# Linear attention, SwiGLU and softplus layers on one core: one more unit's output products by seven, and gate and value partials kept in tiles

## The chip, the cores and the metric

The kernel runs on one core of a Trainium2 chip. The metric is the device time of one execution in microseconds, and of several executions the median. The core's engines run beside each other and wait for one another by semaphores: TensorE (PE, with its weight loads PEld), VectorE (DVE), ScalarE (ACT), GpSimd (POOL) and SyncE (SP), whose queue issues all transfers here.

## The reference, cut to what matters

```python
q_s = softmax(q, axis=-1); k_s = softmax(k, axis=2)           # 4 batches, 8 heads, 576 rows, 64 wide
kv = einsum('bhsd,bhse->bhde', k_s, v)
x = einsum('bhsd,bhde->bhse', q_s, kv)                         # to 2304 tokens x 512
xn = x / sqrt(mean(x * x) + 1e-6) * rms_g
g = xn @ w_gate; val = xn @ w_val                              # 512 -> 1536
x = (g / (1 + exp(-g)) * val) @ w_out                          # first layer, 1536 -> 512
h = x @ w_in                                                   # second layer, 512 -> 2048
out = (maximum(h, 0) + log1p(exp(-abs(h)))) @ w2_out           # softplus, 2048 -> 512
```

## The kernel before, in words

All data are 32-bit floats. To multiply them on TensorE, a tile is cut into two halves, a rounded one (`[:, 0]`) and the rest (`[:, 1]`), and one product is three matmuls (`mm3`, lines 946 to 948): high by high, high by low, low by high. Sums stay in the eight banks of PSUM; `bank()` hands one out.

Tokens are taken in blocks of 384 (T), two blocks to a pair, three pairs. The first layer does a third of its hidden width plainly (steps G, V, S, A, O) and the rest, and the whole second layer, "by seven": a two by two product of blocks is made from seven block products of sums and differences instead of from eight. For that, quadrants of the tokens (`quad_sum`, `quad_h`, `quad_l`) and of the weights (`pair_sum`, `make_h`, `make_l`) are summed and cut in halves ahead of time; weights prepared so are put into DRAM ("kept") and loaded again (`load_b`, line 1291).

A first-layer unit u (12 of them) is one token pair and one pair of hidden chunks. For gate and for value it makes seven products (`a_mul`, step M.u.k.g or M.u.k.v, k from 0 to 6, each six matmuls of 384 columns). Partial sums are copied (`a_copy`, step C, lines 1228 and 1232), added (`a_sum`, D, line 1236), and go through silu (SI, line 1244) and gate (U, line 1252). In the kernel before, product 0 is copied from its bank to a second bank, and product 1 is summed onto that copy; product 3 takes a third bank. The four results are cut in halves (BH, line 1264; BL, line 1268) and multiplied with the output weights onto a copy of the running output (OP, line 1272; OM; OC, line 1281).

A second-layer unit u (0 to 23, eight for each of three token pairs) makes seven products with w_in (`h_mul`, step H), copies and adds partials (HC, line 1306; HD, line 1310), and applies softplus (SP, line 1324). Its output products are either plain (`y_mul`, step Y.u.o.f.t: for two token blocks o, two hidden chunks f and three groups t of 128 tokens, 12 products of three matmuls of 512 columns, summed in six banks over the units) or by seven (`y_part`, step YP.u.k.t: 21 products of three matmuls of 256 columns). By seven needs seven tiles in halves instead of four, four sums of softplus tiles (SU, line 1371), the weights' differences (yc and yd) and, for products 1 to 4, an addition to running totals on chip (YA, line 1409); products 5 to 7 stay in five banks over all units of a token pair. In the end YX (line 1471) joins totals and banks, YS (line 1475) adds what plain units left in banks, and YO stores (lines 1357 and 1360). Which units go by seven stands in `BY7`: before, 4 to 21; units 0 to 3, 22 and 23 are plain.

The front part is the attention: q maxima, exponentials and sums (Q0 line 802, QS 806, QR 824, QM 835), k maxima (K0, line 687), transposes and broadcasts (K1, KM, K2, KS), key by value products (K3), their scaling (K4, lines 786 to 789), the attention output (X0, line 873), and the conversion of weights that come as 64-bit floats (CA, CL line 508, CD lines 514 to 522, CC, CS line 540).

What runs when is written out by hand or by a search: the text ORDER lists about 4,100 steps, and each engine does its own in that order. A step's last letter names the engine where there is a choice (V is DVE, A is ACT, P is POOL). HOMES lists which buffer each tile takes (`ps`: banks; `w`: 16 weight buffers).

Of the kernel before, what the change touches and what calls it, by code (L numbers as in the profile page):

```python
# [27 lines left out]
LQ.0.0 Q0.0.0 LQ.0.1 QS.0.0.1.V LQ.0.2 F.5 QS.0.0.0.P QE.0.0.1 Q0.0.1 Q0.0.2 LK.0.0.1 QE.0.0.0 LK.0.1.1 QS.0.1.0.P  # L28
QS.0.1.1.P MX CA.5.A LK.0.2.2 F.0 QE.0.1.0 QR.0.0 QI.0.0 LX.0 QE.0.1.1 K0.0.0.1.1.V QM.0.0.0.V QS.0.2.0.P QR.0.1 QM.0.0.1.P
K0.0.1.1.1.V K0.0.0.1.2.V K0.0.2.2.1.V F.3 K0.0.0.1.3.V QE.0.2.0 K0.0.2.2.2.V QI.0.1 B.0.33 T.1 CL.5.V K0.0.1.1.2.V F.10 MV  # L30
K0.0.2.2.3.V T.0 LQ.1.0 K0.0.1.1.3.V K0.0.0.1.4.V K0.0.1.1.4.V K0.0.2.2.4.V CA.0.A CL.0.V B.1.6 K1.0.0 CA.3.A LW.0 KM.0.0
B.2.2 K2.0.0 CD.0.0 LV.0.0.4 CL.3.P LV.0.4.8 K1.0.2 QR.0.2.0 QM.0.1.0.P KS.0.0 KE.0.0 QI.0.2.0 KM.0.2 Q0.1.0 QM.0.2.0.P
B.3.7 K2.0.2 TC.1.A KS.0.2 QS.1.0.0.P CD.3.0 CA.10.A CL.10.V QM.0.1.1.V T.2 F.6 CD.0.1 KE.0.2 MK CD.5.0 LK.1.0.2 QE.1.0.0
CD.10.0 CD.3.1 QS.1.0.1.V B.4.4 K3.0.0 LG CD.0.2 K3.0.2 TC.0.A T.3 TC.2.A LK.1.2.2 CD.3.2 K4.0.0 CC.3.A CD.10.1 K4.0.2
QE.1.0.1 QR.1.0 B.5.1 X0.0.1 T.4 X0.0.0 CA.6.A CD.10.2 LX.1 CL.6.V SQ.0.1 LQ.1.1 K0.1.0.2.1.V CD.5.1 CS.3.P SQ.0.0
K0.1.0.2.2.V K0.1.2.2.1.V X0.0.3 X0.0.2 SQ.0.2 SQ.0.3 XG.0.1.A K0.1.0.2.3.V XG.0.0.A X1.0.4.0 K0.1.2.2.2.V XG.0.2.A CC.10.A
CC.0.A X1.0.4.2 K0.1.0.2.4.V K0.1.2.2.3.V QI.1.0 X1.0.4.1 QM.1.0.1.P K0.1.2.2.4.V K1.1.0 LV.1.0.4 KM.1.0 B.6.1 K1.1.2 K2.1.0
XD.0 TC.4.A XP.0 Q0.1.1 XG.0.3.A QM.1.0.0.P KM.1.2 B.7.2 K2.1.2 X2.0 KS.1.0 T.5 KE.1.0 QS.1.1.0.P QS.1.1.1.P QE.1.1.1 LW.1
KS.1.2 F.1 X3.0.1 QE.1.1.0 X3.0.0 HH.0.0.A T.6 CS.10.P KE.1.2 LV.1.4.8 HH.0.1.A TC.3.A TC.5.A LK.2.2.2 X3.0.2 CS.0.V
HH.0.2.A F.7 HL.0.0.P B.8.1 K3.1.0 G.1.0 K3.1.2 QR.1.1 CD.6.0 LQ.2.0 X3.0.3 CA.1.A QI.1.1 QM.1.1.1.V K4.1.0 HH.0.3.A G.0.0  # L40
K4.1.2 X0.1.2 HL.0.1.P X0.1.3 CD.6.1 HL.0.2.P CA.7.A X0.1.0 K0.2.2.2.1.V CD.5.2 K0.2.2.2.2.V CL.7.V X0.1.1 SQ.1.1 XG.1.2.A
T.8 CD.6.2 HL.0.3.V SQ.1.2 CD.7.0 CL.1.V LX.2 SQ.1.0 K0.2.2.2.3.V F.4 CD.7.1 XG.1.1.A SQ.1.3 G.1.1 K0.2.2.2.4.V LK.2.0.2
XS.1.2.3.V G.0.1 G.1.2 XS.1.0.1.V G.0.2 QM.1.1.0.P XG.1.0.A V.3 CA.4.A CC.6.A G.0.3 CD.7.2 T.7 Q0.2.0 G.1.3 XG.1.3.A
K0.2.0.2.1.V CS.6.P TC.7.V K1.2.2 LW.2 G.2.0 S.1 KM.2.2 F.9 XS.1.0.2.P LQ.2.1 TC.6.A TC.8.A S.0 K0.2.0.2.2.V G.2.1 CC.5.A
CL.4.V X1.1 CC.7.A LV.2.0.4 K0.2.0.2.3.V CS.7.P X0.2.1 CD.1.0 K0.2.0.2.4.V X0.2.2 XD.1 CD.4.0 K1.2.0 K2.2.2 KM.2.0 G.2.2
CS.5.P KS.2.2 K2.2.0 KS.2.0 CA.9.A X0.2.3 X0.2.0 CD.1.1 SQ.2.1 SQ.2.2 F.2 KE.2.0 QS.2.0.0.V V.2 CL.9.V CD.1.2 XG.2.1.A
XG.2.0.A LV.2.4.8 QS.2.0.1.V CC.1.A CD.9.0 Q0.2.1 G.2.3 XP.1 X2.1 XG.2.2.A KE.2.2 CD.9.1 SQ.2.0 CD.4.1 K3.2.0 CA.2.A CS.1.P
CD.9.2 CD.4.2 CL.2.V QE.2.0.1 LX.3 F.8 CC.9.A CC.4.A LV.3.0.4 CS.9.V V.0 SQ.2.3 QE.2.0.0 X3.1.0 HH.1.0.A A.0 CS.4.P X3.1.3
XG.2.3.A K3.2.2 S.2 QS.2.1.1.P QR.2.0 G.3.0 K4.2.2 QI.2.0 QS.2.1.0.P AH.0.A V.1 HL.1.0.P HH.1.3.A K4.2.0 G.3.1 X3.1.2 LQ.1.2
X3.1.1 F.11 A.1 QM.2.0.1.P QE.2.1.1 XS.2.0.1.V G.5.0 AH.1.V G.7.0 HH.1.1.A CA.11.A HL.1.1.V G.3.2 QM.2.0.0.P G.4.0 HH.1.2.A  # L50
HL.1.2.V QE.2.1.0 T.10 CL.11.V G.3.3 S.3 G.6.0 G.7.1 CD.2.0 XS.2.2.3.V CA.8.A TC.10.A CD.2.1 LK.3.0.2 Q0.1.2 CL.8.V HL.1.3.V
CD.8.0 AL.1.V AL.0.V CD.2.2 G.7.2 CD.8.1 G.6.1 G.5.1 V.5 A.3 G.5.2 A.2 CC.2.A G.5.3 CD.8.2 T.9 CD.11.0 TC.9.A QS.1.2.0.V
QR.2.1 CD.11.1 K0.3.0.2.1.V S.5 LV.3.4.8 G.4.1 G.4.2 CC.8.A G.6.2 G.4.3 CS.2.P O.0 O.1 S.4 AH.2.A K0.3.0.2.2.V AH.3.A
XS.2.0.2.V X1.2 LQ.3.0 AL.2.V CD.11.2 G.6.3 CS.8.P K0.3.0.2.3.V XD.2 G.7.3 A.5 XP.2 QI.2.1 CC.11.A F.15 LK.3.2.2 V.4 CS.11.V
F.12 K0.3.0.2.4.V Q0.3.0 QM.2.1.0.P S.6 CA.15.A X2.2 AL.3.P X3.2.0 HH.2.0.A O.2 O.3 CA.12.A AH.5.A K1.3.0 CL.15.V A.4 S.7
E.0.2.A CD.15.0 T.11 V.7 X3.2.2 CL.12.V TC.11.A X0.3.0 QM.2.1.1.P X0.3.1 K0.3.2.2.1.V AH.4.V LQ.3.1 E.0.1.A E.0.0.V X0.3.3
KM.3.0 CD.12.0 AL.4.P QE.1.2.0 HL.2.0.P X3.2.1 XG.3.3.A XG.3.0.A QS.3.0.1.V X3.2.3 V.6 X0.3.2 SQ.3.3 Q0.3.1 CD.15.1 AL.5.P
E.0.3.A CD.12.1 A.6 SQ.3.1 O.4 SQ.3.0 AH.6.A K0.3.2.2.2.V HH.2.3.V CD.15.2 CD.12.2 AL.6.V QS.3.1.1.V QS.3.0.0.P ST.15
XG.3.1.A O.5 HH.2.1.V A.7 SQ.3.2 K0.3.2.2.3.V O.6 K2.3.0 QE.3.0.1 G.9.0 AH.7.A XS.3.0.1.P XS.3.2.3.V AL.7.V HH.2.2.A
QE.3.0.0 QE.3.1.1 O.7 XG.3.2.V KS.3.0 XS.3.0.2.P KE.3.0 E.1.0.A ST.12 X1.3 K0.3.2.2.4.V F.14 QR.1.2.0 F.19 HL.2.3.V XD.3  # L60
T.12 HL.2.1.V G.8.0 G.10.0 CA.14.A G.10.1 K1.3.2 G.9.1 CA.19.A G.8.1 HL.2.2.P CL.14.V QR.3.0 CL.19.V CD.14.0 KM.3.2 QI.3.0
LW.3 G.10.2 TC.12.V G.10.3 QI.1.2.0 QM.3.0.0.P QS.3.1.0.P XP.3 V.9 QE.3.1.0 G.9.2 T.14 G.8.2 E.1.2.V G.9.3 G.8.3 QR.3.1
TC.14.A G.11.0 QM.1.2.0.V CD.19.0 S.8 CD.19.1 K2.3.2 K3.3.0 CD.14.1 CD.19.2 F.13 S.9 A.9 KS.3.2 CD.14.2 X2.3 QI.3.1 K4.3.0
V.8 G.11.1 G.11.2 X3.3.3 QM.3.1.1.V QM.3.1.0.V T.13 G.11.3 ST.19 F.16 AH.9.V A.8 KE.3.2 T.16 S.10 QM.3.0.1.P K3.3.2 X3.3.1
AH.8.V X3.3.2 E.1.1.A V.11 K4.3.2 S.11 V.10 TC.13.A CA.13.A ST.14 T.17 CL.13.V X0.4.3 CA.16.V HH.3.1.V CD.13.0 X0.4.2
CL.16.V AL.9.P XG.4.3.A CD.16.0 X3.3.0 X0.4.0 AL.8.P A.10 T.15 SQ.4.3 X0.4.1 CD.13.1 HH.3.2.V SQ.4.2 HH.3.0.A A.11 CD.13.2
E.1.3.A ST.13 TC.17.V CD.16.1 XG.4.2.A XG.4.0.A O.8 TC.15.A SQ.4.0 HH.3.3.V HL.3.0.V CD.16.2 O.9 G.13.0 XG.4.1.A HL.3.1.V
F.18 SQ.4.1 AH.10.A HL.3.3.V XS.4.2.3.P TC.16.V F.17 AL.10.P O.10 AH.11.V AL.11.V X0.5.2 XS.4.0.1.P XS.4.0.2.P X1.4 G.14.0
XD.4 HL.3.2.P O.11 XG.5.2.V XP.4 G.13.1 CA.18.A CL.18.V G.14.1 G.13.2 G.13.3 E.2.0.A X0.5.0 SQ.5.2 ZS.1.t1.P SQ.5.0 CD.18.0
X2.4 S.13 ST.16 G.12.0 XG.5.0.A CA.17.A E.2.1.V G.12.1 CD.18.1 E.2.2.A X3.4.3 ZS.1.t3.P X0.5.3 CD.18.2 X3.4.1 V.12 E.2.3.A  # L70
V.14 X3.4.2 XG.5.3.V SQ.5.3 X0.5.1 ST.18 HH.4.1.A XG.5.1.V XS.5.2.3.P V.15 X3.4.0 V.13 SQ.5.1 G.15.0 G.15.1 HH.4.0.V
HL.4.0.P G.12.2 XS.5.0.1.V XS.5.0.2.P A.13 G.12.3 CL.17.V CD.17.0 X1.5 XD.5 CD.17.1 G.14.2 G.18.0 G.14.3 XP.5 G.19.0 S.12
HH.4.3.A HH.4.2.A G.15.2 S.14 X2.5 A.12 TU.12 HL.4.1.P G.17.0 HL.4.2.V F.22 AH.12.V LATE AL.12.P CD.17.2 WH.12.1.A G.15.3
TU.13 A.14 F.21 ZH.0.22.qe1.A G.16.0 G.16.1 S.15 ST.17 HL.4.3.V G.19.1 G.16.2 AH.13.A X3.5.3 G.19.2 AL.13.P PS.13.0.P G.18.1
ZH.0.11.qe0.V V.19 A.15 AH.14.V AL.14.V CA.21.A G.19.3 G.16.3 X3.5.2 G.17.1 V.17 X3.5.1 PS.13.1.P G.18.2 S.16 G.17.2 G.18.3
CL.21.V HH.5.1.A PS.13.2.V WH.13.2.A AH.15.V ZL.0.22.V S.19 WL.13.2.V CD.21.0 CD.21.1 G.17.3 A.19 CA.22.V WL.12.1.V HH.5.3.A
X3.5.0 CL.22.P AL.15.P V.18 S.17 HL.5.3.P CD.22.0 CD.22.1 PS.13.3.P AH.19.A HL.5.1.V O.12 CD.22.2 CD.21.2 O.13 V.16
WH.13.4.V AL.19.V O.14 WH.13.3.A O.15.0 HH.5.0.A O.15.3 A.16 O.15.2 HL.5.0.P G.20.0 G.20.1 AH.16.V AL.16.V ZS.0.t3.V TU.14
A.17 ST.21 O.16.0 HH.5.2.V HL.5.2.P S.18 V.20 TU.15 E.3.3.A PS.15.0.P G.20.2 G.20.3 ST.22 AH.17.V G.21.0 AL.17.V A.18
PS.15.1.P WH.14.1.V F.20 G.23.0 E.3.0.V PS.15.2.V ZL.0.11.V E.3.2.V G.21.1 WH.15.2.V F.23 S.20 A.20 G.21.2 O.16.3 WL.14.1.V  # L80
G.23.1 PS.15.3.V O.16.2 AH.18.A G.22.0 WL.15.2.V O.17.2 CA.23.A WL.13.3.V O.17.3 G.21.3 TU.16 ZS.0.t1.V G.22.1 AL.18.V
G.22.2 CL.23.P O.15.1 O.16.1 CD.23.0 CA.20.V E.3.1.V G.23.2 CD.23.1 AH.20.A CL.20.V CD.23.2 ST.23 G.22.3 S.22 ZH.0.21.hl.V
# [260 lines left out]
ps 3630365756452437170231547546252162513523223623322632636266234063023564  # L343
qh 01010101
qm2_ 01010101
raw 01010101011010101001010110101010101010101001010101001010101010100011010101100101011101101010
qs2_ 01201201
mx 01010101
qn 012102010210210210
# [19 lines left out]
def linear_attention_swiglu_softplus_kernel(  # L369
# [23 lines left out]
    T = 384  # L393
# [51 lines left out]
    def bank():  # L445
        return take(ps_p, "ps", [P, 512])
# [1136 lines left out]
```

## Time and profile before

| | |
|---|---|
| median of 3 runs | 885.22 us (885.11 to 886.08) |
| the profiled execution | 885.05 us |
| its span, from first to last instruction | 883.3 us |
| granted TensorE clock, mean | 0.996 |
| busy: PE, PEld, DVE, ACT, POOL | 867.8, 846.6, 759.4, 446.2, 321.7 us |
| matmuls | 5360 |

The span is what the profile shows of the profiled execution; its own time is 1.75 us longer. Busy time counts an engine's instructions; matmuls overlap each other, and their ends are modelled.

### The profile page before, as it was taken

How to read it: one execution, taken by the hardware profiler on the slowest of the kernel's cores; microseconds unless marked ns; L12 is line 12 of the kernel's file. 1: busy time of each engine (PE TensorE's matmuls, PEld its weight loads, DVE VectorE, ACT ScalarE, POOL GpSimd, SP SyncE). 2: the span in 40 equal slices, each digit the busy share in tenths (PEclk: the TensorE clock that was granted, in tenths of full speed). 3: DMA queues.
4: the chain of work that ended last, by engine and by line, in shares of the span. 5: the costliest groups of instructions: out<-in, count | busy, mean ns of one | idle time of the engine just before them, and what ended most of it. 6: DMA issues, size and time to landing. Idle time of an engine off the chain costs nothing.

```text
span 883.3 us, 15104 instructions
## 1 busy us (share of the span) xinstructions
PE 867.8 (98%) x5360; PEld 846.6 (96%) x5360; DVE 759.4 (86%) x1444; ACT 446.2 (51%) x888; POOL 321.7 (36%) x286
## 2 busy tenths in 40 slices
PE   7899999999999999999999999999999999999997
PEld 7789999999999999999999998999999999999996
DVE  7999988488898899998999999899998786877774
ACT  3578555232576654655556776757653323232220
POOL 5443522452405133131333224135325335364321
PEclk9899999999999999999999999999999999999999
DMA  9996324113889897898898989898979887678832
GB/s 259 206 250 162 96 78 127 65 49 118 297 333 362 283 349 269 306 336 323 293 359 301 351 303 339 320 323 309 333 237 341 270 292 257 211 243 298 280 100 72
DMA packets 119803, 223.03 MB, mean 253 GB/s; under 512 B 31024, under 2 KB 75824, under 8 KB 119728
## 3 DMA queue, kind: packets, MB, share of 16 engines
q1 hardware_dynamic: 119728, 222.07, 75.3%
q8 instruction: 42, 0.69, 0.3%
q14 instruction: 33, 0.27, 0.1%
HBM read 166.20 MB, written 55.84 MB: 251 GB/s over the span
## 4 chain that ended last, share of the span: by engine, by line
PE 82%; DVE 10%; DMA 5%; issue 2%; ACT 1%; SPq 0%; POOL 0%; DVEq 0%; ACTq 0%
PE ps L946 26%; PE ps L947 26%; PE ps L948 26%; DMA raw<-in_moe_w_out_dram 2%; PE ps L873 2%; PE ps L778 1%; DMA raw<-in_moe_w_in_dram 1%; DVE h L1268 1%; DVE bits L518 1%; DMA out_dram<-x 1%; DMA kept<-ws 1%; PE ps L901 1%; DMA qx<-in_q_dram 1%; PE ps L843 1%; DVE a L1252 1%
## 5 line engine op out<-in xcount | busy, mean ns | idle before, releaser
L946 PE MATMUL ps<-hl,w 128*128 128x384 f32 x280 | 97.1, 347 | 0.0
L947 PE MATMUL ps<-hl,w 128*128 128x384 f32 x280 | 93.8, 335 | 0.0
L948 PE MATMUL ps<-hl,w 128*128 128x384 f32 x280 | 93.8, 335 | 0.0
L946 PE MATMUL ps<-xy,w 128*128 128x384 f32 x256 | 86.5, 338 | 0.7 <-DVE s L1310 0.3
L947 PE MATMUL ps<-xy,w 128*128 128x384 f32 x256 | 85.9, 335 | 0.0
L948 PE MATMUL ps<-xy,w 128*128 128x384 f32 x256 | 85.8, 335 | 0.0
L1409 DVE TENSOR_TENSOR x<-ps,x 128x512 f32<-128x512 f32 x96 | 64.6, 683 | 16.9 <-PE ps L948 15.6
L946 PE MATMUL ps<-w,h 128*128 128x256 f32 (+1 forms) x198 | 59.2, 299 | 0.0
L948 PE MATMUL ps<-w,h 128*128 128x256 f32 (+1 forms) x198 | 59.2, 299 | 0.0
L947 PE MATMUL ps<-w,h 128*128 128x256 f32 (+1 forms) x198 | 59.1, 299 | 0.0
L946 PE MATMUL ps<-h,w 128*128 128x384 f32 x168 | 56.7, 338 | 0.0
L947 PE MATMUL ps<-h,w 128*128 128x384 f32 x168 | 56.3, 335 | 0.4 <-DVE h L1268 0.4
L948 PE MATMUL ps<-h,w 128*128 128x384 f32 x168 | 56.2, 334 | 0.0
L946 PEld LDWEIGHTS ps<-hl,w 128*128 128x128 f32 x280 | 52.6, 188 | 1.0 <-ACT s L1017 0.3
L947 PEld LDWEIGHTS ps<-hl,w 128*128 128x128 f32 x280 | 52.7, 188 | 0.7
L948 PEld LDWEIGHTS ps<-hl,w 128*128 128x128 f32 x280 | 52.6, 188 | 0.0
L946 PEld LDWEIGHTS ps<-xy,w 128*128 128x128 f32 x256 | 48.1, 188 | 2.4 <-ACT ln L1232 0.6
L503 ACT ACTIVATE bits<-raw 128x512 f32<-128x512 f32 x54 | 36.2, 673 | 26.9 <-DMA raw<-in_moe_w_out_dram 9.0
L947 PEld LDWEIGHTS ps<-xy,w 128*128 128x128 f32 x256 | 48.2, 188 | 0.4
L948 PEld LDWEIGHTS ps<-xy,w 128*128 128x128 f32 x256 | 48.1, 188 | 0.0
L518 DVE SCALAR_TENSOR_TENSOR bits<-raw,bits 128x512 int32<-128x512 int32 x62 | 46.8, 758 | 0.8
L522 DVE SCALAR_TENSOR_TENSOR bits<-raw,bits 128x512 int32<-128x512 int32 x62 | 44.8, 730 | 0.6
(534 smaller groups left out, 2918.5 us busy)
## 6 DMA issues: line engine op xcount, KB each, us to landing
w<-kept SPq DMA_DIRECT2D x90, 512.0 KB, 5.4
kept<-ws SPq DMA_DIRECT2D x48, 512.0 KB, 5.3
xy<-outside SPq DMA_DIRECT2D x22, 768.0 KB, 6.9
raw<-in_moe_w_out_dram SPq DMA_DIRECT2D x26, 512.0 KB, 5.0
hl<-outside SPq DMA_DIRECT2D x24, 384.0 KB, 6.9
raw<-in_moe_w_in_dram SPq DMA_DIRECT2D x16, 512.0 KB, 5.2
outside<-hl SPq DMA_DIRECT2D x18, 384.0 KB, 5.3
qe<-outside SPq DMA_DIRECT2D x8, 768.0 KB, 9.0
```

The costliest lines, as they stand in the source:

```text
L503: nc.scalar.activation(out=b.bitcast(F32), in_=hi, func=AF.Abs)
L518: nc.vector.scalar_tensor_tensor(out=b, in0=words[:, :, 1], scalar=-0x40000000, in1=b, op0=ALU.bitwise_and, op1=ALU.bitwise_or)
L522: nc.vector.scalar_tensor_tensor(out=b, in0=words[:, :, 0], scalar=29, in1=b, op0=ALU.logical_shift_right, op1=ALU.bitwise_or)
L778: nc.tensor.matmul(out=ps[:, i, :], lhsT=ke_t[lo][:, i, r], rhs=v_t[:, m, r, :], start=(r == 0), stop=(r == R))
L843: nc.tensor.transpose(ps[:, m * P:(m + 1) * P], t[:, m * P:(m + 1) * P], ident)
L873: nc.tensor.matmul(out=ps[:, s:s + n], lhsT=kvb[b % 2][:, m, :], rhs=qT_t[:, m, s:s + n], start=True, stop=True)
L901: nc.tensor.matmul(out=rs[j][:, c:c + 1], lhsT=sq_t[:, m, c * P:(c + 1) * P], rhs=ones, start=m == 0, stop=m == n - 1)
L946: nc.tensor.matmul(out=ps, lhsT=wh, rhs=xh, start=first, stop=False, skip_group_check=more)
L947: nc.tensor.matmul(out=ps, lhsT=wh, rhs=xl, start=False, stop=False, skip_group_check=more)
L948: nc.tensor.matmul(out=ps, lhsT=wl, rhs=xh, start=False, stop=last, skip_group_check=more)
L1252: nc.vector.tensor_tensor(out=t, in0=part.pop((u, k, "g")), in1=src, op=ALU.mult)
L1409: nc.vector.tensor_tensor(out=tot, in0=ybank.pop((u, pair, t)), in1=tot, op=ALU.add)
```

## The change

Four things change. Unit 22 joins `BY7`, so its 12 plain output products become 21 products by seven; only unit 23 is still plain. In `a_mul` products 0 and 1 each take a fresh bank, and product 3 starts anew in the bank of product 1; the copy of product 0 goes to a tile on chip, and a new step D.u.1 adds product 1 to it there, so that silu and gate of that result read tiles instead of a bank. K0 of the first heads of batches 0 and 2 is one reduction over all rows instead of four maxima (the letter R; only the step with r = 1 issues an instruction). And ORDER and HOMES are new as a whole: nearly every step stands at another place, and many change engine. On DVE there are 13 fewer OC, 11 fewer OP, 5 fewer C, 14 fewer BH, 16 fewer BL; POOL has 19 more BL.

```diff
         def a_mul(u, k, n):
...
-            if k in (0, 3):
+            if k < 2:
                 bk[u, n, b] = bank()[:, :T]
             w = wt[("x4" if wn == "x4" else n + wn, p)]
-            at = bk[u, n, 2 if k == 1 else b]
-            seven(at, w, off + (256 * "gv".index(n) if wn == "x4" else 0), quad[r, xname], new and k != 1)
+            seven(bk[u, n, b], w, off + (256 * "gv".index(n) if wn == "x4" else 0), quad[r, xname], new)
 
         def a_copy(u, k, n, e):
-            if k == 0:
-                bk[u, n, 2] = bank()[:, :T]
-                copy[e](out=bk[u, n, 2], in_=bk[u, n, 0])
-                return
             tag = "ln" if k == 2 else {"g": "s", "v": "a"}[n]
...
         def a_silu(u, k):
-            if k in (4, 5):
+            if k < 6:
...
-                src = bk[u, "g", 2 if k == 1 else 0]
+                src = bk[u, "g", SEVEN[k][3]]
...
         def a_gate(u, k):
-            if k in (4, 5):
+            if k < 6:
...
-                src = bk[u, "v", 2 if k == 1 else 0]
+                src = bk[u, "v", SEVEN[k][3]]
...
-        BY7 = set(range(TURN, 2 * NPB)) | set(range(2 * NPB, 3 * NPB - 2))
+        BY7 = set(range(TURN, 3 * NPB - 1))
...
         def y_mul(u, o, f, t, half=None):
...
-            first = p == (NPB - 2 if i == 2 else 0) and f == o
+            first = (jp, o, t) not in acc
...
-            more = half is not None
-            last = p == (NPB if i else TURN) - 1 or (p == NPB - 2 and (i, o, t) == (2, 0, NCB - 1))
-            mm3(acc[jp, o, t][:, n], h[:, 0, c], h[:, 1, c], w[:, 0, n], w[:, 1, n], first, last and f != o, more)
+            mm3(acc[jp, o, t][:, n], h[:, 0, c], h[:, 1, c], w[:, 0, n], w[:, 1, n], first, p == (NPB if i else TURN) - 1 and f != o, True)
```

The end of the new ORDER, from the last H product on:

```
H.23.6 SP.23.1.0 YP.22.5.2 YA.22.0.1 YX.2.0.0.P
YP.22.6.0 BL.34.2.3.V YX.2.1.0.V YP.22.7.0 BH.35.1.1.A SP.23.0.0 YP.22.3.0 YP.21.3.0 BL.34.1.1.P BH.35.1.0.A YX.2.0.1.V
YP.21.4.2 BH.35.0.0.A BL.35.1.1.P YP.21.4.0 YP.22.4.1 YP.22.7.2 YX.2.0.2.V YA.21.1.0 YX.2.1.1.V BL.35.1.0.P BL.35.0.0.P
YP.22.7.1 YP.21.3.2 YA.21.1.2 BH.35.0.1.A YP.22.4.0 YP.22.3.2 YP.22.3.1 YA.22.1.0 YP.22.4.2 YX.2.1.2.V YA.22.1.1 Y.23.1.1.1
YA.22.1.2 Y.23.0.0.1 YX.2.0.4.V Y.23.0.0.0 Y.23.0.1.0 Y.23.0.0.2.1 YX.2.1.4.V YX.2.0.3.P YS.0.0.0 BL.35.0.1.P Y.23.1.1.2
Y.23.0.1.1 YX.2.0.6.V Y.23.0.0.2.0 Y.23.1.0.1 YO.0.0.0 Y.23.0.1.2.1 Y.23.0.1.2.0 YS.0.0.1 YO.0.0.1 YX.2.0.5.P YS.0.1.1
YO.0.1.1 YX.2.1.6.V YX.2.1.3.V YX.2.1.5.P YS.0.0.2.0 YO.0.0.2.0 Y.23.1.0.2 Y.23.1.1.0 YS.0.0.2.1 YO.0.0.2.1 YS.0.1.2
Y.23.1.0.0 YS.0.1.0 YO.0.1.2 YO.0.1.0
```

## Rows read from the trace of the kernel before

**Rows 1.** Page, busy time of each engine, share of the span, instructions.

```profile
PE 867.8 (98%) x5360; PEld 846.6 (96%) x5360; DVE 759.4 (86%) x1444; ACT 446.2 (51%) x888; POOL 321.7 (36%) x286
```

**Rows 2.** Windows: stretch, busy PE, PEld, DVE, ACT, POOL, granted clock, DMA share, GB/s.

```profile
0.00:50.00 50.00, 42.31 (x290) 39.18 (x291) 44.05 (x92) 26.00 (x43) 25.81 (x31) 0.93 0.96 237
...
37.00:43.80 6.80, 6.80 (x33) 6.45 (x33) 6.65 (x15) 3.38 (x6) 5.41 (x6) 0.50 0.74 164
...
226.00:515.00 289.00, 287.83 (x1652) 285.60 (x1651) 261.18 (x498) 173.88 (x371) 86.79 (x74) 1.00 0.89 321
...
860.00:884.00 24.00, 18.21 (x92) 15.35 (x90) 10.96 (x19) 1.43 (x3) 3.29 (x3) 0.99 0.21 67
```

**Rows 3.** Waits of PE past the start: total us, times, longest.

```profile
PE ps L947 <- DVE h L1268: 0.4, 1, 0.4
...
PE ps L946 <- ACT ln L1232: 0.3, 1, 0.3
```

**Rows 4.** Timeline of PE at 411.5 us: start, length, instruction, idle before.

```profile
411.50 0.34 PE L948 MATMUL ps<-xy,w 128*128 128x384 f32 x1
412.21 0.44 PE L946 MATMUL ps<-xy,wf 128*128 128x384 f32 x1 [0.36 <-DVE a L1252]
```

**Rows 5.** Timeline of PE: three matmuls of 256 columns, nine of 512.

```profile
654.58 0.28 PE L948 MATMUL ps<-wc,raw 128*128 128x256 f32 x1
...
654.94 0.28 PE L948 MATMUL ps<-wc,raw 128*128 128x256 f32 x1
...
871.55 0.39 PE L946 MATMUL ps<-we,h 128*128 128x512 f32 x1
...
873.59 0.39 PE L946 MATMUL ps<-wf,h 128*128 128x512 f32 x1
```

**Rows 6.** Instructions by line: ns min/median/max, first and last start, forms.

```profile
L518 DVE SCALAR_TENSOR_TENSOR bits<-raw,bits x62: 672/685/1656, 30.1 to 610.4; 128x512 int32<-128x512 int32 x62
...
L518 DVE SCALAR_TENSOR_TENSOR bits<-raw,bits x1: 1561/1561/1561, 30.1 to 30.1; 128x512 int32<-128x512 int32 x1
...
L1268 DVE TENSOR_TENSOR h<-s,h x36: 542/549/1094, 516.6 to 856.3; 128x384 fp32r<-128x384 f32 x36
...
L1268 POOL TENSOR_TENSOR h<-a,h x15: 1008/1020/1468, 281.3 to 865.8; 128x384 fp32r<-128x384 f32 x15
...
L1409 DVE TENSOR_TENSOR x<-ps,x x96: 671/682/693, 597.3 to 858.9; 128x512 f32<-128x512 f32 x96
...
L1475 DVE TENSOR_TENSOR x<-ps,x x7: 416/678/692, 870.4 to 878.2; 128x512 f32<-128x512 f32 x5, 128x256 f32<-128x256 f32 x2
```

**Rows 7.** Groups by shape: busy us, mean ns, idle before.

```profile
L1281 DVE COPY x<-ps 128x384 f32<-128x384 f32 x35 | 18.9, 548 | 3.0 <-PE ps L948 3.0
...
L1236 DVE TENSOR_TENSOR a<-ps,a 128x384 f32<-128x384 f32 x12 | 6.6, 547 | 1.2 <-PE ps L948 1.2
...
L1471 POOL TENSOR_TENSOR x<-x,x 128x512 f32<-128x512 f32 x3 | 4.2, 1413 | 0.5 <-DVE x L1409 0.5
```

**Rows 8.** The chain that ended last, in the start: start, us on it, what.

```profile
9.12 1.14 DVE qs L824
...
10.89 0.60 DVE qn L835
...
15.71 1.02 DVE km_t L687 x4
...
17.74 0.59 DVE qs L824
...
51.69 2.54 PE ps L873 x14
```

**Rows 9.** DMA issues of weights: count, KB, median us to landing.

```profile
w<-kept SPq DMA_DIRECT2D x90, 512.0 KB, 5.4
```

**Rows 10.** Timeline of the last six microseconds.

```profile
877.82 0.39 PE L948 MATMUL ps<-we,h 128*128 128x512 f32 x1
878.25 0.69 DVE L1475 TENSOR_TENSOR x<-ps,x 128x512 f32<-128x512 f32 x1 [0.60 <-PE ps L948]
878.96 0.46 SPq L1360 DMA_DIRECT2D out_dram<-x  x1
```

**Rows 11.** Timeline of POOL at 30 us.

```profile
29.88 1.28 POOL L540 TENSOR_TENSOR w<-x,w 128x512 fp32r<-128x512 f32 x1 [5.62 <-ACT w L536]
```

## What I expect of it

> **What bounds the kernel now.** I read the page first. TensorE is busy for 98% of the span, the DVE for 86%, ACT and POOL far less [rows 1]. A busy PE on the page is not a PE at its peak, so I read two more views. The windows show where PE is not full [rows 2]: it lacks 7.7 us of the first 50 us and 5.8 us of the last 24; in the long stretch of the first layer's sevens it lacks 1.2 us of 289. In the start DVE is as full as PE: between 37 and 43.8 us it is busy 6.65 of 6.80 us, while PE is granted 0.50 of its clock (1.2 of 2.4 GHz). Then the waits of PE [rows 3]: past the start the view lists four of 0.3 to 0.4 us, of which the largest and the smallest stand there. Matmuls overlap, so such a wait costs a little more than the view says: in the timeline the matmul behind the 0.36 us wait starts 0.71 us after its predecessor [rows 4], where the stretch's mean distance is 289 / 1652 = 0.17, so 0.54 is lost. With that correction the four cost some 2.1 us. So the time is the sum of the start-to-start distances of 5,360 matmuls, plus some 14 us at both ends, plus 2 us of waits. A change gains by taking columns from PE, by a shorter start or end, or out of these 2 us, and by nothing else.
>
> **The products of unit 22.** Removed are the 12 plain products of unit 22, each three matmuls of 512 columns: 36 matmuls. From the first to the tenth matmul of a run of such ones is 2.04 us, so 227 ns each [rows 5], 8.17 us together. Added are 21 products of three matmuls of 256 columns: 63, at 0.36 us for three, 120 ns each [rows 5], 7.56 us; read 0.01 us shorter, as the view rounds, it would be 117 ns and 7.35 us. PE gains 0.6 to 0.8 us, I take **-0.7**. Break-even is 8.17 / 63 = 130 ns.
>
> What pays for it is off PE: three more tiles in halves (three BH, three BL), four SU, six YA. A YA is 0.68 us on DVE, six are 4.1 us; a BL or SU is 0.55 us on DVE or 1.02 us on POOL [rows 6]. All fall in the last 40 us, where DVE still has room, 11 of 24 us in the last window [rows 2]. Two weight loads are added (yc and yd of this unit) and one is halved.
>
> **Partials from tiles.** PE does the same products in a_mul. Before, the first partial was copied from bank to bank and the second product was added onto the copy; now the copy goes to a tile and a DVE add (D, step 1) joins the two. That adds 24 DVE adds of 0.55 us [rows 7], 13.2 us in the 289 us stretch, in which DVE is 261 us busy. The new order moves work off DVE in the same stretch: 13 output copies back (OC), 11 output begins (OP) and 5 partial copies to ACT, 29 x 0.55 = 15.9 us at the price of the output copy [rows 7]. DVE is no fuller than it was; ACT, 174 of 289 us busy [rows 2], takes it. I cost this at **0**, with ACT's idle time as cover. Waits change places: gone is product 1 behind the copy of product 0, new is product 3 behind the add that empties its bank (before, product 3 had a fresh bank). In the new order at least two products of six matmuls, 2 x 6 x 0.17 = 2.1 us, stand between products 1 and 3 in each of the 24 cases; the old order left the same 2.1 us at the least between products 0 and 1. An add of 0.55 us fits, if DVE comes to it within 1.5 us. The next product on PE's queue, and all behind it, would wait if not.
>
> The rest of the stretch is the order's: up to 2.1 us of waits can go, one of them (0.54 us, a bank held until DVE's gate had read it) of the kind that the edit frees. As many can come. I take **-0.5**, a quarter of them, since 24 banks fewer are held, with -2.1 and +2.5 as ends (the upper: each of the four and one more, at the largest).
>
> **The start.** The order is new here too. Dense work begins when DVE has finished the second batch's K4 and the X0 matmuls follow at 51.69 us [rows 8]. I count DVE's steps up to that point in both orders. Gone: four maxima of 128x128 at about 0.25 (four such steps, one of them larger, take 1.02), a QM, a QS and a CS at 0.60 each, as the chain shows for a QM [rows 8]: 2.8 us. New: one maximum reduced over all five rows at once (640 elements, which the trace has not; between the 0.59 us of a reduction of 512 and the 1.14 us of one of 1,024 elements [rows 8], near the first: 0.75), a clamp (CL) and a step CD at most at the same 0.60, and a QM: 2.55 us at most. So DVE is 0.3 to 0.5 us ahead. But two G products (three matmuls each, some 0.6 us), which PE did before in its waits ahead of that point, now stand behind it: 1.2 us later on PE. I take **+0.2**. Ends: -1.2 (up to the first batch's K4.0.2 the same count has one more QS and one more CD gone, 1.2 us, and nothing gives it back) and +3.4 (a stretch at half clock of 6.8 us that falls where PE, not DVE, is the chain: half of 6.8).
>
> **Loads.** Between the last reader of a weight buffer and the first use of its next content most loads have over 8 us of PE work in both orders, but WB.23.hx3 goes into a buffer that H.22.5 reads last, and H.23.2 wants it 6.3 us of PE work later; such a load lands 5.4 us after its issue in the median [rows 9], and the load of y0 stands just ahead of it on SP's queue. In the old order the tightest of the last units had 7.3 us. I take **+0.2**, ends 0 and +1.8 (half as long again, since it shares the engines with y0's load: 8.1 less 6.3).
>
> **The end.** Before, PE's last matmul starts at 877.82, the last YS at 878.25, and the last store, issued at 878.96, lasts up to the end of the span at 883.3 [rows 10]. That chain is unchanged. New is what stands ahead of it: unit 22 keeps five banks until its own end, so the YX joins fall in the last 13 us. From the end of H.23.5 PE has 1 H product, 26 of 0.35, 10 plain ones of 0.68 and 4 half ones of 0.35: 18.3 us. DVE has in that time 8 YA, 4 large YX and 4 large YS at 0.68, 6 small YX and 2 small YS at 0.42 [rows 6], 2 HD and 2 BL at 0.55 and a BH of about 0.4: 16.9 us. Two ends of it are close: Y.23.0.0.0 takes the bank that YA.22.1.1 empties, which I find about 0.2 us ahead, and POOL does YX.2.0.0 at 1.41 [rows 7] and BL.34.1.1 at 1.02 after a YA of 0.68, 3.1 us, where PE reaches the product that wants them after 3.8 us. I take **+0.3**, ends 0 and +1.0.
>
> **Sum.** -0.7 - 0.5 + 0.2 + 0.2 + 0.3 = -0.5 against the profiled execution's 885.05 (span 883.3 and 1.75 around it): 884.55. The median of the runs is 885.22, 0.17 above it, so **884.7**.
>
> **Rival 1, faster: the waits go.** The new order loses its waits in the middle (-2.1), the start keeps the 1.2 us by which the first batch comes earlier, and the end costs nothing: 885.2 - 0.7 - 2.1 - 1.2 = 881.2; half of both gives 882.9. For it: PE is the bound almost everywhere, and the bank waits get fewer causes, since a unit holds two banks for each of gate and value instead of three. Against: an order that fits better in one place is tighter elsewhere, as the load above.
>
> **Rival 2, slower: POOL blocks DVE in the end.** 19 more BL run on POOL. A DVE instruction with two operands on chip shows what that can do: L518, 0.69 us in the median, took 1.56 us at 30.14, where a POOL subtraction had begun at 29.88 that lasts 1.28 us [rows 6, 11]; the BL of DVE have a median of 0.55 and a maximum of 1.09 [rows 6]. The Trainium skill, SBUF — State Buffer, section "Who interferes with whom", states this as a rule: of a VectorE instruction with two SBUF inputs and a GpSimd one that reads SBUF the second blocks until the first is done; by that rule, and the trace agrees with 1.56 for 0.69, each move to POOL is a risk for DVE. In the last 18 us DVE has 1.4 us to spare and four to five such instructions (two BL, two joins) beside six POOL ones. Each blocking costs 0.5 to 0.9 us of DVE; the first two go into the spare time, each further one goes to the end. Four and the bank wait behind them: 885.2 - 0.7 + 4 x 0.9 - 1.4 + 1.0 = 887.7. It decides from four blockings on (three give 886.8); that POOL is busy only some 36% of the time speaks against it.
>
> **Rival 3: the gain isn't there.** The 63 short matmuls come at 130 ns instead of 120, because each needs a weight load of its own for half the columns: 885.2.
>
> **Chances.** Forecast 0.47, rival 1 0.30, rival 2 0.10, new waits at the upper ends of the load and the middle (above 887) 0.05, rival 3 0.05, half clock on PE's chain 0.03. What a measurement of this kernel can tell from no change is about 0.2%, 1.8 us. Rival 1 and a little of the forecast fall under 883.4: faster 0.32. Rival 2, the new waits and the clock, and a little of the forecast: slower 0.19. The rest, 0.49, is no change. The forecast's own range is 883.2 to 886.4; for 8 in 10 it reaches to the middle of rivals 1 and 2: 881.8 to 887.3.
>
> **What would show it.** Right: 36 fewer matmuls of 512 columns and 63 more of 256, at 117 to 120 ns; 24 more L1236 adds; no bank-to-bank copies of L1228; the X0 matmuls of the second batch within 1 us of 51.7; last matmul to end of span 5 us as before. Wrong: PE waits over 0.5 us in the list, by DVE adds of L1236 (the new bank wait) or by w<-kept at H.23.2; DVE without gaps in the last 18 us and PE waiting for YA or YX there; a stretch of 0.5 clock at another place.

## The result, and the profile after

The kernel after takes **890.44 us** (median of 4 runs, 889.49 to 891.42); the kernel before took 885.16 us beside it (4 runs). The ratio is 1.0059, 95% interval 1.0045 to 1.0072: 5.3 us slower, clear of noise and outside the predicted range. The profiled execution has a span of 889.2 us, 5.9 more than that of before.

The page of the kernel after, busy time, answers to [rows 1]:

```profile
PE 868.2 (98%) x5391; PEld 847.3 (95%) x5391; DVE 757.2 (85%) x1399; ACT 480.3 (54%) x955; POOL 336.2 (38%) x306
```

Windows of the kernel after, columns as in [rows 2]; the second line is now the stretch at half clock, which lies one microsecond earlier:

```profile
0.00:50.00 50.00, 42.62 (x295) 39.01 (x296) 42.40 (x91) 24.96 (x42) 24.69 (x31) 0.93 0.99 242
36.02:42.85 6.83, 6.83 (x32) 6.37 (x32) 5.33 (x12) 2.95 (x5) 5.67 (x6) 0.50 1.07 225
226.00:515.00 289.00, 284.93 (x1635) 282.83 (x1634) 262.42 (x495) 182.33 (x391) 74.63 (x64) 1.00 0.88 313
...
866.40:884.40 18.00, 18.00 (x121) 16.48 (x120) 15.87 (x29) 4.09 (x9) 9.87 (x9) 1.00 0.12 39
```

In the 289 us stretch PE is now without work for 4.1 us where it was 1.2, though no engine is fuller than the prediction had it: DVE 262 us (before 261), POOL 75 (87), ACT 182 (174, and it was to take more). The last 18 us are as tight as forecast, DVE 15.9 of 18, and PE is busy in all of them. So the loss is neither in the start nor in the end. The list of PE's waits from 180 to 860 us of the kernel after says where it is (engine, line and what is waited for: us in total, times, longest). The whole list for before has four lines of one wait each, 0.4, 0.4, 0.3 and 0.3 us. Two of them stand in [rows 3], these are the others:

```profile
PE ps L946 <- DVE a L1252: 0.4, 1, 0.4
PE ps L946 <- DVE s L1310: 0.3, 1, 0.3
```

And the whole list for after:

```profile
PE ps L949 <- DVE s L1308: 1.6, 2, 1.4
PE ps L949 <- DVE s L1304: 1.3, 1, 1.3
PE ps L949 <- DVE ln L1230: 1.0, 1, 1.0
PE ps L950 <- POOL hl L1178: 0.8, 1, 0.8
PE ps L950 <- POOL hl L946: 0.6, 1, 0.6
PE ps L949 <- ACT x L1279: 0.6, 1, 0.6
PE ps L949 <- DVE x L1456: 0.5, 1, 0.5
PE ps L949 <- ACT hl L938: 0.4, 1, 0.4
PE ps L949 <- DMA xy<-outside: 0.3, 1, 0.3
PE ps L949 <- DVE a L1308: 0.2, 1, 0.2
PE ps L949 <- DVE x L1405: 0.2, 1, 0.2
```

Twelve waits, 7.5 us, where there were four, 1.4 us: 6.1 us more, and the span grew by 5.9. By place, 1.0 us of the list lies between 180 and 226 us (before none), 4.0 in the 289 us stretch (before 1.1) and 2.5 in the second layer, up to 860 us (before 0.3). No line names L1234, the new add. Counted by the distance between two matmuls' starts, as in [rows 4], the twelve come to 9.7 us; the expectations below use that count and have 9.9. Six of them, 6.0 us by that count, stand right behind a DVE or POOL instruction that lasted far longer than others of its form while the other of the two engines worked. The timeline of the kernel after shows the largest:

```profile
600.03 1.30 POOL L608 TENSOR_TENSOR ws<-bits,ws 128x512 fp32r<-128x512 f32 x1 [0.50 <-ACT ws L602]
...
600.41 1.34 DVE L1266 TENSOR_TENSOR h<-s,h 128x384 fp32r<-128x384 f32 x1 [1.06 <-ACT h L1262]
...
600.92 0.28 PE L951 MATMUL ps<-wf,h 128*128 128x256 f32 x1
...
602.00 0.54 DVE L1308 TENSOR_TENSOR s<-ps,s 128x384 f32<-128x384 f32 x1
...
602.60 0.44 PE L949 MATMUL ps<-xy,wd 128*128 128x384 f32 x1 [1.40 <-DVE s L1308]
```

The BL on DVE takes 1.34 us instead of 0.55 [rows 6] and ends just after the POOL subtraction that began before it. HD.6.1 behind it empties the bank in which product 3 of unit 6 (H.6.3) begins, and PE stands for 1.40 us. The same picture, with a copy instead of an add, at M.8.4.v:

```profile
426.50 1.78 DVE L608 TENSOR_TENSOR ws<-bits,ws 128x512 fp32r<-128x512 f32 x1
428.21 0.55 DVE L1234 TENSOR_TENSOR ln<-ps,ln 128x384 f32<-128x384 f32 x1
428.67 0.54 DVE L1230 COPY ln<-ps 128x384 f32<-128x384 f32 x1
...
426.29 1.44 POOL L608 TENSOR_TENSOR wd<-bits,wd 128x512 fp32r<-128x512 f32 x1 [1.87 <-ACT wd L602]
...
429.27 0.44 PE L949 MATMUL ps<-xy,w 128*128 128x384 f32 x1 [1.03 <-DVE ln L1230]
```

From this came theory **A**: POOL beside DVE makes the loss. Its rival **B**: DVE is late there whoever else works. Later came **C**: each wait is a place where the order puts a step too near to what it waits for, whatever made that late. Its rival **B'**: the engines are behind on the whole, so a wait that is taken away comes back at the next product.

### The profile page after: what moved, and what is told of

It reads as the page before. It is cut to its first block, busy times and chain, and to the rows that moved or that the text cites. A ratio compares the mean times of both kernels' runs of the same rounds, so it can differ in the third digit from the quotient of the medians.

```text
span 889.2 us, 15215 instructions
## 1 busy us (share of the span) xinstructions
PE 868.2 (98%) x5391; PEld 847.3 (95%) x5391; DVE 757.2 (85%) x1399; ACT 480.3 (54%) x955; POOL 336.2 (38%) x306
## 4 chain that ended last, share of the span: by engine, by line
PE 78%; DVE 11%; DMA 4%; issue 3%; POOL 2%; ACT 1%; SPq 0%; POOLq 0%; DVEq 0%; ACTq 0%
PE ps L949 25%; PE ps L950 24%; PE ps L951 24%; DMA kept<-ws 2%; PE ps L876 2%; DMA xy<-outside 1%; DVE xy L723 1%; DVE bits L521 1%; DVE x L1405 1%; PE ps L846 1%; DMA w<-kept 1%; PE ps L904 1%; DVE qs L827 1%; DVE bits L525 1%; PE ps L781 1%
## 5 line engine op out<-in xcount | busy, mean ns | idle before, releaser
L1405 DVE TENSOR_TENSOR x<-ps,x 128x512 f32<-128x512 f32 x102 | 68.4, 684 | 24.8 <-PE ps L951 24.4
L949 PE MATMUL ps<-w,h 128*128 128x256 f32 (+1 forms) x248 | 75.7, 305 | 0.3 <-DVE a L1308 0.2
L951 PE MATMUL ps<-w,h 128*128 128x256 f32 (+1 forms) x248 | 75.9, 306 | 0.0
L950 PE MATMUL ps<-w,h 128*128 128x256 f32 (+1 forms) x248 | 75.7, 305 | 0.0
L949 PE MATMUL ps<-xy,w 128*128 128x384 f32 x216 | 72.8, 337 | 2.6 <-DVE s L1304 1.3
L950 PE MATMUL ps<-xy,w 128*128 128x384 f32 x216 | 72.4, 335 | 0.0
L951 PE MATMUL ps<-xy,w 128*128 128x384 f32 x216 | 72.3, 335 | 0.0
L1279 ACT COPY x<-ps 128x384 f32<-128x384 f32 x74 | 35.0, 482 | 27.1 <-PE ps L951 27.1
L506 ACT ACTIVATE bits<-raw 128x512 f32<-128x512 f32 x58 | 39.1, 676 | 19.2 <-DMA raw<-in_moe_w_out_dram 5.5
L949 PEld LDWEIGHTS ps<-w,h 128*128 128x128 f32 x248 | 46.9, 189 | 2.5 <-issue 0.5
L951 PEld LDWEIGHTS ps<-w,h 128*128 128x128 f32 x248 | 47.0, 190 | 2.1
L950 PEld LDWEIGHTS ps<-w,h 128*128 128x128 f32 x248 | 47.0, 189 | 1.4
L525 DVE SCALAR_TENSOR_TENSOR bits<-raw,bits 128x512 int32<-128x512 int32 x62 | 46.2, 745 | 0.8
```

Source lines behind the costliest of these rows:

```text
L506: nc.scalar.activation(out=b.bitcast(F32), in_=hi, func=AF.Abs)
L525: nc.vector.scalar_tensor_tensor(out=b, in0=words[:, :, 0], scalar=29, in1=b, op0=ALU.logical_shift_right, op1=ALU.bitwise_or)
L949: nc.tensor.matmul(out=ps, lhsT=wh, rhs=xh, start=first, stop=False, skip_group_check=more)
L950: nc.tensor.matmul(out=ps, lhsT=wh, rhs=xl, start=False, stop=False, skip_group_check=more)
L951: nc.tensor.matmul(out=ps, lhsT=wl, rhs=xh, start=False, stop=last, skip_group_check=more)
L1279: copy[e](out=x2t[2 * RUNS[RUN_OF[u]][1] + o][:, m], in_=acc.pop((u, o, m)))
```

## The experiments

All are the kernel after with the edit named, unless it says otherwise. Ratios are to the kernel before on the same chip, with 95% intervals; a difference of ratios is turned into us with 885.

**Seven POOL steps to DVE.** They are the ones beside the six waits.

```diff
-ZL.1.t1.P WL.42.1.P VL.0.1.P VA.1.1.P WL.65.2.P ZS.10.t4.P BL.25.1.0.P
+ZL.1.t1.V WL.42.1.V VL.0.1.V VA.1.1.V WL.65.2.V ZS.10.t4.V BL.25.1.0.V
```

> The kernel after, with seven of its POOL steps done by DVE at the same places (ZL.1.t1, WL.42.1, VL.0.1, VA.1.1, WL.65.2, ZS.10.t4, BL.25.1.0): those that run beside a stretched DVE or POOL instruction just ahead of six of the PE waits of after (258.6, 427.9, 507.0, 600.9, 634.3 and 728.2 us; 1.01 + 1.20 + 1.49 + 1.56 + 0.41 + 0.33 = 6.0 us). Theory A (POOL and DVE block each other, and the blocked instruction is what PE waits for): the six waits shrink to 1.5 us or less, 884.5 to 887. Theory B (DVE is merely late there, whoever else works): seven more DVE instructions, 0.55 to 1.1 us each, make it later: 890 to 893.

Measured: 891.37 us, ratio 1.0067 (1.0044 to 1.0091). In its profile four of the six waits are gone and two are down to 0.2 us, but others stand elsewhere, one of 2.0 us behind an ACT copy (PE stands from 637 us on). The time is the one that B gave, yet the places behaved as A said.

**Seven others as a control.**

```diff
-ZL.0.t2.P WL.28.1.P WL.39.1.P VL.2.0.P VA.5.1.P ZS.11.t4.P BL.28.1.0.P
+ZL.0.t2.V WL.28.1.V WL.39.1.V VL.2.0.V VA.5.1.V ZS.11.t4.V BL.28.1.0.V
```

> The kernel after, with seven other POOL steps of the same families done by DVE, at places where PE does not wait (ZL.0.t2, WL.28.1, WL.39.1, VL.2.0, VA.5.1, ZS.11.t4, BL.28.1.0). Theory A: the six waits stay, 889.5 to 891.5. If fewer POOL steps help wherever they are (POOL's mean load is the cause), it gains as much as the run that moves the seven beside the waits, 884.5 to 887. Theory B: as after or later, 890 to 893.

Measured: 891.92 us, 1.0070 (1.0054 to 1.0087). One of the six waits (427.9 us) is gone though its neighbours stayed on POOL, and new ones of 0.4 to 0.8 us (from start to start) came at 380, 462, 490 and 545 us. A move of work to DVE gains nothing in either place.

**The engines of one order under the other.** A sample of the 580 changed letters (they don't stand beside each other in ORDER), in the order of after:

```diff
-OP.3.1.0.A BL.4.0.0.V OP.3.0.2.V C.5.0.g.V WH.32.1.A
+OP.3.1.0.V BL.4.0.0.P OP.3.0.2.A C.5.0.g.A WH.32.1.V
```

> The order of after, with the engine of every step that both kernels have taken from the kernel before (580 steps change engine). If the new engine choice alone makes the loss and the new order is as good as the old: 884 to 886. If order and engines only fit each other (a search's result is a whole): over 892, with waits of PE at new places. Theory A says no number here, but that the waits stand behind stretched instructions.

Measured: 984.13 us, 1.112 (1.1104 to 1.1137), with 52 waits of PE in the list from 180 to 860 us.

The reverse, 580 letters of after put into the order of before:

> The kernel before (its code and its order), with the engines of after (580 steps change engine). If the new engine choice makes the loss: about 890. If order and engines only fit each other: over 888 and more than after, with waits at new places.

Measured: 949.80 us, 1.0724 (1.0708 to 1.074), 37 waits. An order and its engine choice only work together; the new engine choice cannot be blamed by itself.

**The seven steps kept on POOL, but short.**

```diff
+            out, in0, in1 = (t[:, :8] if len(t.shape) == 2 else t[:, :, :8] for t in (out, in0, in1))
             nc.gpsimd.tensor_tensor(out=out, in0=in0, in1=in1, op=op)
```

> The kernel after, with the seven POOL steps of the first run left on POOL but cut to 8 columns (the rest of their results is left out), so that they neither last nor give DVE more work. Theory A (the six waits come from POOL running beside DVE just there): the six waits, 6.0 us together, go and nothing takes their place, 884 to 886. Theory B (DVE or the queues are late there for other reasons): 889 to 890.5. If the waits go and others come behind them, so that the time stays over 888, the schedule as a whole is tight and a single place decides nothing.

Measured: 888.05 us, 1.0034 (1.0018 to 1.0049); nine waits, 3.6 us. Five of the six waits are gone in the profiled execution and the sixth is down to 0.4, its span is 4.5 us shorter; the ratio fell by 0.0025, some 2.2 us, with intervals that just touch (that of after begins at 1.0045). A's 884 to 886 is missed; the third outcome fits, others come in their place and the time stays over 888. So these stretched instructions do seem to cost time, but less than half of what the change lost. The next two ask the same of more of POOL's steps.

**Most of POOL's steps short, in both kernels.** Nine kinds of steps are cut in this way, each buffer's first one excepted. POOL isn't empty by it, as the expectations have it, but between 226 and 860 us it is busy for 125 us instead of 231 in after, and for 132 instead of 224 in before:

```diff
+            n = 8 if (out.name, out.offset) in full else out.shape[-1]
+            full.add((out.name, out.offset))
+            out, in0, in1 = (t[:, :n] if len(t.shape) == 2 else t[:, :, :n] for t in (out, in0, in1))
             nc.gpsimd.tensor_tensor(out=out, in0=in0, in1=in1, op=op)
```

> The kernel after, with POOL's steps of the kinds BL, SU, WL, VS, VL, VA, ZL, ZS and YX from the first M step on cut to 8 columns wherever the buffer has been written once (188 steps less those first ones): POOL is nearly empty, its results are left out. Theory A: of the 9.9 us of waits past 180 us those that stand behind a stretched or late POOL or DVE instruction go, some 7 us: 882 to 884.5. Theory B: 889 to 891. The difference to the same cut in the kernel before tells what the new order loses by POOL.

> The kernel before with the same cut (170 steps). Its waits past 180 us are 2 to 4 us and one of them at the most stands behind a stretched instruction. Theory A: 882.5 to 885. Theory B: as before, 885. If both kernels with the cut agree within 1 us, all of the loss of after hangs on POOL; if after stays 4 us or more above, none does.

Measured: after with the cut 887.81 us, 1.0038 (1.0018 to 1.0059); before with the cut 883.00 us, 0.9975 (0.9963 to 0.9986). So the cut returns 2 us in both kernels (in before clear of noise, in after within intervals that overlap), and 5.6 us (0.0063 of 885; 4.8 by the medians) still lie between them. The list of waits of before with the cut is this:

```profile
PE ps L952 <- DVE a L1258: 0.4, 1, 0.4
PE ps L952 <- DVE x L992: 0.2, 1, 0.2
```

That of after with the cut has nine lines, of which the first five:

```profile
PE ps L957 <- POOL hl L431: 0.9, 1, 0.9
PE ps L957 <- POOL hl L953: 0.6, 1, 0.6
PE ps L956 <- ACT x L1286: 0.6, 1, 0.6
PE ps L956 <- ACT a L1311: 0.5, 1, 0.5
PE ps L956 <- ACT hl L945: 0.4, 1, 0.4
```

The two POOL steps named here are of those that were not cut (an HL, and the first ZL into its buffer), 1.5 us of waits; the others stand behind ACT, DVE or a load. Even without those two, 3 to 4 us would lie between the kernels. Theory A falls as the account of the whole difference, though after's 887.81 lies in neither theory's range.

**The 24 new adds short.**

```diff
+            c = slice(0, 8) if k == 1 else slice(0, T)
-            nc.vector.tensor_tensor(out=t, in0=bk[u, n, SEVEN[k][3]], in1=t, op=ALU.add)
+            nc.vector.tensor_tensor(out=t[:, c], in0=bk[u, n, SEVEN[k][3]][:, c], in1=t[:, c], op=ALU.add)
```

> The kernel after, with the 24 new adds (D, step 1) cut to 8 columns; the rest of their results is left out. That takes 24 x 0.48 = 11.5 us of DVE's work out of the stretch from 180 to 515 us. If the edit itself, priced at nothing, makes the loss (DVE is too full with the adds): 885 to 886.5. Theory A (other places): 889 to 890.5, with the six waits where they were, but for those behind an add.

Measured: 888.54 us, 1.0042 (1.0025 to 1.0059), eleven waits, 5.9 us. The 24 short adds took 0.15 us each, so 9.6 us less of DVE, and the time fell by 1.5 us, with intervals that overlap that of after. The adds are not the loss, though they are perhaps not quite free.

**Steps moved within the order.** Thirteen steps, each by a few places, no work and no engine changed. The core of it, with steps between left out at `...` (M.5.1.g, H.10.1, H.14.4, HD.8.5 and WL.45.1 are moved alike):

```diff
-M.1.3.v M.1.3.g OM.0.0.2 ... M.1.2.v
+M.1.2.v OM.0.0.2 M.1.3.v M.1.3.g
-H.0.0 ZL.9.21.V OM.10.0.3 ... ZL.9.t1.V U.11.6 H.0.1 HC.0.0.V HD.0.1 H.0.2 ... H.0.3 OM.10.1.1
+OM.10.0.3 H.0.0 ZL.9.21.V ... HC.0.0.V ZL.9.t1.V U.11.6 H.0.1 HD.0.1 H.0.2 ... OM.10.1.1 H.0.3
-H.6.3 H.6.2 YP.4.6.2
+H.6.2 YP.4.6.2 H.6.3
-H.8.2 ... H.8.3 ... YP.6.6.2
+H.8.2 ... YP.6.6.2 H.8.3
-ZH.0.11.qe0.A G.12.1 HH.4.1.A HL.4.1.P ... HH.4.2.A
+G.12.1 HH.4.1.A HL.4.1.P ... HH.4.2.A ZH.0.11.qe0.A
```

> The kernel after with 13 steps moved by a few places in the order, each at one of its ten waits past 180 us; no engine, no work and no buffer changes. On PE a product that needs nothing late goes ahead of the product that waits (or that one goes behind its successor); on DVE the copy or add that PE waits for goes ahead of a step that is not urgent (C.8.2.v ahead of WL.45.1, HC.0.0 ahead of ZL.9.t1, HD.8.5 ahead of ZL.10.t4); on ACT ZH.0.11 goes behind HH.4.2. Theory C (the loss is the order's: some ten places where a step comes 0.3 to 1.6 us late, whatever made it late): most of 9.9 us of waits go and little comes in their place, 882 to 886. Theory B' (PE waits because the other engines are behind on the whole, so a wait that is taken away comes back at the next product): 889 to 891.

Measured: 886.43 us, 1.0007 (0.9997 to 1.0018): 4.6 us of the 5.3 are back. (HC.0.0 takes its tile here before U.11.6 has read it, which changes one tile of unit 11; the later versions put it behind U.11.6.) All twelve waits are gone from the list, and six others, 2.4 us together, have come:

```profile
PE ps L946 <- DVE x L1402: 0.7, 2, 0.4
PE ps L946 <- DVE ln L1305: 0.7, 1, 0.7
PE ps L946 <- ACT x L1398: 0.5, 1, 0.5
PE ps L946 <- DVE ps L1267: 0.3, 1, 0.3
PE ps L946 <- DVE s L1305: 0.2, 1, 0.2
```

Up to 515 us the list falls from 5.0 us to 0.5 (the last two lines), so C holds there. In the second layer it falls only from 2.5 to 1.9 (the first three): there four waits came back elsewhere, as B' had it. With 886.43 the time is just above C's 882 to 886 and far from B''s 889 to 891.

The second layer's part of it alone:

> The same moves in the second layer alone (H.6.3, H.8.3, HD.8.5, H.10.1, H.14.4: the waits at 600.9, 634.3, 640.2, 659.4 and 728.2 us, 3.3 us together). Theory C: 887 to 888.5, the first layer's waits as they were. Theory B': as after.

Measured: 891.15 us, 1.0066 (1.0043 to 1.0090). The span of its profiled execution is 1.9 us shorter than that of after, but the median of four runs (889.2 to 893.3), of which the profiled one is the fastest, shows no gain: a miss for C, which had 887 to 888.5, and what B' had said. On the same chip the thirteen moves together took 886.43, so what they gained is the gain of the other eight, at the waits up to 515 us.

**More moves.** Four versions follow on this one, each with the largest waits of the last one's profile mended in the same way, 17 steps moved in the first, 23 in the second and 22 in the third:

```diff
-VS.1.1.P BH.12.0.0.A OP.11.0.3.A VS.1.3.V OP.10.1.0.V
+VS.1.1.P BH.12.0.0.A OP.11.0.3.A OP.10.1.0.V VS.1.3.V
-CA.51.A CD.52.2 OP.8.1.0.A
+OP.8.1.0.A CA.51.A CD.52.2
-SP.2.0.0 BH.14.0.0.A ... HC.2.2.A
+HC.2.2.A SP.2.0.0 BH.14.0.0.A
-WL.65.3.V YA.4.0.0 HC.6.2.A VK.4.0 YA.4.1.1
+YA.4.0.0 HC.6.2.A VK.4.0 YA.4.1.1 WL.65.3.V
-H.0.2 OP.10.1.3.A U.11.4 D.11.5.v OM.10.1.1 H.0.3
+OM.10.1.1 H.0.2 OP.10.1.3.A U.11.4 D.11.5.v H.0.3
```

> The moves of the run with 13 moved steps, but HC.0.0 behind U.11.6 (it takes a tile that U.11.6 still reads) and without the move of H.14.4, and five more at the waits which that run still had: OP.10.1.0 ahead of VS.1.3 on DVE; H.0.5, H.8.6, YP.4.2.0 and YP.9.1.2 behind products that follow them. Theory C: 883 to 886, waits past 180 us over 0.25 us under 4 us in sum. Theory B' (waits come back elsewhere): 887 to 889.

Measured: 886.24 us, 1.0018 (1.0006 to 1.0029); five waits, 3.0 us. It lies between C's range and B''s. With HC.0.0 behind U.11.6, then, 3.6 us of the 5.3 are back.

> The run before with six more steps moved, at the four largest waits that it still had (0.75, 0.72, 0.61 and 1.35 us) and one of 0.31: OP.8.1.0 ahead of CA.51 and HC.2.2 ahead of SP.2.0.0 on ACT, WL.65.3 behind YA.4.1.1, ZL.10.t4 behind YA.6.0.0 and BL.24.2.4 behind YA.11.1.2 on DVE, YP.6.2.2 behind YP.6.3.1 on PE. Theory C: 3 us less waiting than the run before, 883 to 884.5, so at or just under the kernel before. Theory B' (waits come back elsewhere): 885.5 to 887.

Measured: 886.47 us, 1.0019 (1.0003 to 1.0035), though the profiled execution has a span of only 882.4 us with four waits, 1.9 us. Its runs lie between 884.4 and 892.1, so executions of this order differ by more than the waits that were mended. A miss for C's number; B' had 885.5 to 887.

> The run before, with BL.24.2.4 back at its place (a wait of 0.90 us stood behind its POOL neighbour after the move), H.8.6 behind YP.6.2.2 (0.82 us) and OM.10.1.1 ahead of H.0.2 (0.45 us). Theory C: 884.5 to 886. Theory B' (the time stays where the moves brought it, whatever single wait is taken away): 886 to 887.

Measured: **885.23 us, 1.0003 (0.9994 to 1.0012)**, in C's range. The list of waits of this kernel:

```profile
PE ps L947 <- DVE h L1263: 0.9, 2, 0.6
PE ps L946 <- DVE ps L1267: 0.8, 1, 0.8
PE ps L946 <- DVE x L1402: 0.4, 2, 0.2
```

And the place that stood 1.03 us in the kernel after, in the timeline of this one:

```profile
424.06 0.55 DVE L1227 COPY ln<-ps 128x384 f32<-128x384 f32 x1
...
424.52 1.02 DVE L605 TENSOR_TENSOR ws<-bits,ws 128x512 fp32r<-128x512 f32 x1
...
425.46 0.33 PE L946 MATMUL ps<-xy,w 128*128 128x384 f32 x1
```

The copy C.8.2.v now stands ahead of WL.45.1. The subtraction is still stretched by POOL (1.02 us, 0.69 when alone), and nothing waits for it: M.8.4.v starts at 425.46 without idle time. By the ratio all but 0.3 us of the loss is back, give or take 0.8 (by the medians on this chip, 885.23 and 884.43, all but 0.8), with the same instructions on the same engines.

**POOL cut in the mended order**, the edit of the two cut kernels:

> The same order with POOL's steps cut to 8 columns as in the two cut runs (their results are left out). The cut took 2 us from both kernels. If what is left over the kernel before (1.7 us) is POOL beside DVE, the cut takes it too: 882 to 883, level with the cut kernel before or 0.7 us under it. If order and POOL are two names for the same waits: 884 to 886.

Measured: 883.42 us, 0.9992 (0.9980 to 1.0005): 1.0 us (0.0011 of 885) under the same order uncut, 1.5 us (0.0017) above before with the cut, where the uncut pair is 0.3 us apart; the intervals of these differences are as wide as they are, and the time lies between the two expectations. Nothing here speaks for POOL as what keeps the mended order from gaining.

**Two more moves**, OM.6.0.3 and OM.11.0.0 (the 20 moves of the expectation are the 22 of the run before the last):

> The run with 20 moves, with two more on PE: OM.6.0.3 behind M.7.2.v (it waited 0.97 and 0.73 us for DVE) and OM.11.0.0 behind OM.10.1.2 (0.63 us). Theory C: 883.5 to 884.6, so under the kernel before by what the products of unit 22 save (0.7 us) or a little less. If the moves have reached their end: 885 to 886.

Measured: 885.23 us, 1.0003 (0.9993 to 1.0013). The moves have reached their end, as the second expectation had it; no version with all its work in it is faster than the kernel before.

Set side by side, single profiled executions of the kernels with all their work, or all but a few steps of it, show how far the span follows the list of waits (all in us). The last column lies between 880.5 and 883.8; it also holds the start, which differs between executions: the first waiting product past 180 us starts at 181.07 in after and at 180.15 in the run of the second layer's moves, with the same order up to there.

| kernel | span | waits listed, 180 to 860 us | span less waits |
|---|---|---|---|
| before | 883.3 | 1.4 (4) | 881.9 |
| after | 889.2 | 7.5 (12) | 881.7 |
| seven POOL steps to DVE | 891.8 | 8.2 (14) | 883.6 |
| seven others to DVE | 890.6 | 6.8 (12) | 883.8 |
| seven short | 884.7 | 3.6 (9) | 881.1 |
| new adds short | 888.0 | 5.9 (11) | 882.1 |
| 13 steps moved | 884.9 | 2.4 (6) | 882.5 |
| the second layer's 5 alone | 887.3 | 6.6 (9) | 880.7 |
| 17 steps moved | 886.0 | 3.0 (5) | 883.0 |
| 23 steps moved | 882.4 | 1.9 (4) | 880.5 |
| 22 steps moved | 883.8 | 2.1 (5) | 881.7 |
| two more | 885.7 | 2.0 (5) | 883.7 |

## Why the prediction was wrong

**Unit 22's products: right.** In the trace of after there are 1,209 matmuls of 256 columns (before 1,146) and 174 of 512 (210). From start to start the 63 of unit 22 take 7.54 us in all, the 36 of before 8.27 (120 and 230 ns each): 0.73 us, the term of the sum (-0.7). Twelve of 256 columns in the timeline of after, 1.44 us from the first to the thirteenth:

```profile
867.77 0.28 PE L949 MATMUL ps<-w,raw 128*128 128x256 f32 x1
...
869.21 0.28 PE L949 MATMUL ps<-w,h 128*128 128x256 f32 x1
```

**Partials from tiles, at 0: right as far as the runs tell.** The 24 adds are there, 12 more on each of these two rows than before, and cost 0.55 us each:

```profile
L1234 DVE TENSOR_TENSOR s<-ps,s x24: 537/550/558, 233.3 to 499.0; 128x384 f32<-128x384 f32 x24
L1234 DVE TENSOR_TENSOR a<-ps,a x24: 540/550/558, 235.6 to 500.1; 128x384 f32<-128x384 f32 x24
```

The new bank wait, product 3 behind its add, is in no line of the list. Taking the adds away returned 1.5 us, which the intervals do not tell from nothing, and the mended order is level with before with all adds in it.

**The start, loads, the end: right or a little too dear.** PE's X0 matmuls follow DVE's K4 at 51.74 us, before at 51.69 [rows 8], the half-clock stretch is 6.83 us long (before 6.80 [rows 2]) and costs the same. H.23.2 does not wait for its load. The last matmul starts at 884.09 and the span ends 5.1 us later, before 5.5 [rows 10]: 0.4 us gained instead of 0.3 lost. Rival 2 did not come in the end, where it was placed: behind the wait at 728.7 us the list has none. (In the working of the start, 2.8 less 2.55 is 0.25, not 0.3 to 0.5; nothing hangs on it.)

```profile
51.74 0.76 PE L876 MATMUL ps<-qT_t,kvb 128*128 128x192 f32 x3 [1.13 <-DVE kvb L792]
...
884.09 0.39 PE L951 MATMUL ps<-w,h 128*128 128x512 f32 x1
```

**The step that failed** is the last one under "Partials from tiles": the rest of the stretch "is the order's", -0.5, with +2.5 as the upper end, "each of the four and one more, at the largest". It measured +6.1 in the lists: +2.9 in the stretch that the term names, +1.0 ahead of it and +2.2 in the second layer, where the sum had no term (one of the four waits of before, at 655.5 us, lies there too, outside the stretch). The bound took the number and the size of the waits in the old order for those of a new one. Nothing in the rows of before limits how many places of a new order are tight; only its own margins do. The working did count one of these, the add of 0.55 us that fits "if DVE comes to it within 1.5 us", and stopped at the 24 cases that the edit made new.

Four of the twelve waits, 3.9 us in the first three lines of the list, are of just that kind, but not new with the edit: a product that accumulates onto, or begins in, a bank that a copy or an add must read first (M.8.4.v, H.0.2, H.6.3, H.8.3). Counted from the two ORDER texts with 0.17 us for a matmul of 384 columns and 0.36 for a YP, 2.1, 2.1, 1.8 and 1.4 us of PE work stand between these products and the ones whose result must be read first; in before it was 6.2, 4.2, 3.5 and 2.5. In these four DVE came later than that, because an instruction ahead of it in DVE's order was stretched to 1.3 to 2.6 us while POOL worked. The other eight wait for other things: halves that ACT or POOL made late (at 180 us behind a less urgent ACT step, at 259 us behind a stretched POOL step), a bank that an ACT copy or a DVE add had still to empty, a load. The 22 moves show that places in the order are what was lost: they alone, with the same work on the same engines, brought the time back. They do not show that short margins alone make a wait: the shortest four between products 1 and 3 of a second-layer unit are 1.0, 1.1, 1.1 and 1.4 us in before, and 1.0, 1.0, 1.0 and 1.1 in after.

**Rival 2's mechanism is real, its place was wrong, and it is not the difference.** A DVE or POOL instruction stretched beside the other engine stands ahead of six of the twelve waits, in the middle. The Trainium skill, SBUF — State Buffer, section "Who interferes with whom", says that of a VectorE instruction with two SBUF inputs and a GpSimd one that reads SBUF the second blocks until the first is done. The traces agree in the two places shown: the DVE subtraction that starts at 426.50 ends 0.55 us after POOL's, which ends at 427.73, and the BL that starts at 600.41 ends 0.42 us after POOL's, which ends at 601.33. But with POOL's steps short both kernels gain 2 us, so what POOL costs, both orders pay; whether PE pays more is decided by what stands behind the stretched instruction.

**The other rivals.** Rival 1 is the failed step with the other sign: the waits did not go, they came. Rival 3 fell with the 120 ns.

**What stays open.** The 0.7 us of unit 22's products came out in no median. The mended order still lists 2.1 us of waits against 1.4, which would be just that, but these are single executions. Nor is it known whether another order would bring the gain, or whether moves of this kind would make the kernel before faster too: none were tried on it. The new buffer list (HOMES) is at least not where the loss lies: the mended order keeps it as it is.

## What to carry to other kernels

When a change brings a new order, the old order's waits give no bound for it: list each product that accumulates onto something copied or added by another engine, and set its distance in PE work against that engine's queue with one stretched instruction (here 1.3 to 2.6 us) in it. (That such a list would have found these places beforehand was not tried.) When such an order comes out slower, read PE's list of waits first and move single steps, the waiting product behind its successor or the awaited copy ahead of work that nobody waits for: 17 moves gave back 3.6 and 22 moves 5.0 of 5.3 us here, while shortening or moving other engines' work gave 0 to 2. And judge such mends by the median of several runs, since one profiled execution may flatter them by 2 us.

## What had not been expected of the hardware

Executions of one order can differ by more than the change is worth: twelve of one mended order lay between 884.4 and 892.1 us (all but one under 888.7), those of the kernel before beside it between 883.9 and 887.4; those of the last but one version were closer, 883.4 to 886.2. And mending the four largest waits that one profile listed, worth 3 us, left the median where it was (886.24 and 886.47). An order also holds only with the engines that it came with: exchanging the engine of 580 steps out of some 4,100 for those of the other kernel, with the same steps to do, cost 11% in one order and 7% in the other, against the 0.6% of the whole change.
